# Six last tiles with transfers and PV of their own, and output stores in whole tiles, in a grouped-query attention kernel

## The chip, the core and the metric

One core of a Trainium2 chip. The metric is device time in microseconds (us) of one execution. A profiled execution gives a trace; its "span" runs from the first to the last instruction of the program.

## What is computed

Attention without a mask, 16 batches, 32 query heads over 8 key heads, 16 queries, 2048 keys, head width 128, in bf16:

```
B, Hq, Hkv, Sq, Sk, D = 16, 32, 8, 16, 2048, 128
k = jnp.repeat(k, Hq // Hkv, axis=1); v = jnp.repeat(v, Hq // Hkv, axis=1)
scores = jnp.einsum("bhqd,bhkd->bhqk", q, k) * D ** -0.5
return jnp.einsum("bhqk,bhkd->bhqd", softmax(scores), v)
```

Each of the 128 key heads has 64 query rows. K and V are 64 MB each and are read once; the output is 2 MB.

## The kernel before, in words

**Tiles.** Two key heads make a *tile*: 128 query rows by 2048 keys. There are 64 tiles (0 to 63); two tiles make a *quad* (0 to 31), that is four heads, numbered by g and i. Tile 2d+i holds the two heads (g = 0, 1) of quad d with the same i. A *turn* is four tiles (`STEP`), a *round* eight (`ROUND`).

**One tile's way.** SP (`load_k`) brings K, 1 MB, into one of eight slots of `Kd`. DVE (`kt`) transposes the slot to `KT`. PE (`scores`) writes `S_ps`. DVE scales it to `Sneg` and finds the row bound. ACT (`exp`) writes P and the row sums. PE (`turn_p`) transposes P into `ST_ps`, ACT (`p_out`) copies that to `PT`. PE (`pv`) multiplies by V. P of a quad's two tiles is interleaved, so `pv` works on a quad: two halves of 64 matmuls, each with 64 rows and 64 columns of the array. ACT multiplies the result by the reciprocal of the row sum into `Osb` (DVE does so for the last quads).

**What sets the order.** All transfers go through SP's one queue, written out by hand: for each t from 0 to 70, K of tile t, then stores of an earlier quad, with V of tile p between them where p + `v_lag(p)` = t (a lag of 7 for the late tiles). An instruction that waits holds all behind it. `load_v` waits until PE has finished with the quad that used the buffer before (`sem_pv`; two V buffers of a quad each). `load_k` waits for the transpose of the tile eight before. The V of the last two quads (tiles 60 to 63) goes to slots 0 to 3 of `Kd`, which have no more K by then; that of tiles 62 and 63 is cut in pieces (`LAST_V`). Quads 0 to 27 are stored inside this order, in four transfers of 64 rows each; quads 28 to 31 behind the last V (line 232 on), in two transfers each:

```
    dst = of[d, :, g].rearrange("i x d -> x i d")
    sp.dma_start(dst, Osb[d % NO][64 * g:64 * (g + 1), :, :]).then_inc(sem_o[d % NO], 16)
```

PE, DVE and ACT run loops with the first and last rounds written out; PE's loop has 17 passes (the last for two halves of `pv` alone), and behind it stand the turns of tiles 62 and 63 and the PV of quads 30 and 31.

## Time and profile before

| | |
|---|---|
| median of 3 runs | 343.06 us (342.91 to 343.24) |
| the profiled execution | 342.74 us |
| its span | 340.8 us, so 1.94 us lie around it |
| busy share of the span | DVE 86%, PE 83%, ACT 77% |
| granted PE clock, mean | 0.972 |
| read from HBM, written | 136.31 MB, 2.10 MB |

The profile gives, for each engine, what it did and what ended its idle time; the DMA rows give the share of time in which the 16 DMA engines moved packets, and the rate. The trace further holds a record of each DMA packet (start, duration, size) and of each semaphore increment by a DMA engine, here called a *landing*: every transfer ends with one 4-byte packet on each DMA engine that took part.

### The profile page before, as it was taken

The numbers are of one execution on the slowest core, as the hardware profiler recorded it, in microseconds if no ns is written. First come the engines' busy times: TensorE is split into PE (matmuls) and PEld (weight loads), VectorE is DVE, ScalarE is ACT, GpSimd is POOL, SyncE is SP. The second block draws the span as 40 slices with busy tenths as digits, with TensorE's granted clock in tenths as the row PEclk, the third lists the DMA queues.
The fourth block names the chain that finished last, engine by engine and source line by source line (L and its number), as shares of the span: only waits on it lengthen the run. The fifth ranks groups of instructions, "written<-read, shape, count | busy, mean of one in ns | idle before, by whom it ended". The sixth has DMA issues, their size and how long they took to land.

```text
span 340.8 us, 15409 instructions
## 1 busy us (share of the span) xinstructions
PE 282.6 (83%) x6912; PEld 164.6 (48%) x6912; DVE 293.7 (86%) x265; ACT 261.2 (77%) x349; POOL 31.3 (9%) x22
## 2 busy tenths in 40 slices
PE   1655888888979888998898888988999789897973
PEld 1322445544555455554554554545554544553663
DVE  2999899999989999999989999999999898898611
ACT  2465888888868888988878888888888698787760
POOL 3202020200102020100202020010202010000000
PEclk9857799999999999999999999999999999999998
DMA  7999999999999999999999999999999999999993
GB/s 274 426 418 418 417 418 420 422 420 422 423 423 412 410 425 382 419 422 421 424 421 422 424 422 422 422 422 421 422 423 423 420 423 425 425 420 423 333 414 114
DMA packets 31434, 138.55 MB, mean 407 GB/s; under 512 B 12480, under 2 KB 14784, under 8 KB 15296
## 3 DMA queue, kind: packets, MB, share of 16 engines
q1 hardware_dynamic: 31424, 138.43, 99.2%
q8 instruction: 5, 0.08, 0.1%
q14 instruction: 5, 0.04, 0.0%
HBM read 136.31 MB, written 2.10 MB: 406 GB/s over the span
## 4 chain that ended last, share of the span: by engine, by line
PE 38%; DMA 25%; ACT 20%; issue 7%; DVE 5%; SPq 5%; ACTq 0%
DMA Vd<-in_v_dram 23%; PE S_ps L268 15%; PE ST_ps L279 11%; ACT P L456 11%; PE O_ps L289 10%; ACT PT L465 4%; DVE Sneg L403 3%; ACT O L495 2%; ACT QT L447 2%; SPq L217 2%; DMA Kd<-in_k_dram 2%; DVE KT L395 2%; PE S_ps L289 2%; SPq L183 1%; SPq L202 1%
## 5 line engine op out<-in xcount | busy, mean ns | idle before, releaser
L456 ACT ACTIVATE P<-Sneg,nbias 128x2048 bf16<-128x2048 f32 (+1 forms) x65 | 160.6, 2471 | 4.2 <-DVE Sneg L403 4.2
L403 DVE TENSOR_SCALAR_CACHE_REDUCE Sneg<-S_ps 128x2048 f32<-128x2048 f32 x64 | 145.2, 2269 | 17.5 <-PE S_ps L268 17.4
L395 DVE STREAM_TRANSPOSE KT<-Kd 128x2048 f32<-128x2048 f32 x64 | 147.0, 2298 | 13.6 <-DMA Kd<-in_k_dram 13.6
L268 PE MATMUL S_ps<-KT,QT 32*64 32x512 bf16 x2048 | 127.8, 624 | 21.9 <-DVE Sneg L403 18.9
L465 ACT ACTIVATE PT<-ST_ps 128x512 f32<-128x512 f32 x128 | 69.7, 595 | 55.5 <-PE ST_ps L279 55.5
L279 PE MATMUL ST_ps<-ident,P 128*128 128x128 f32 x512 | 70.2, 281 | 18.5 <-ACT QT L447 10.7
L289 PEld LDWEIGHTS O_ps<-Vd,PT 64*64 64x64 bf16 x3840 | 56.1, 107 | 36.7 <-issue 35.3
L289 PE MATMUL O_ps<-Vd,PT 64*64 64x128 bf16 x3840 | 65.3, 218 | 7.4 <-DMA Vd<-in_v_dram 7.3
L279 PEld LDWEIGHTS ST_ps<-ident,P 128*128 128x128 f32 x512 | 55.3, 142 | 27.7 <-issue 24.0
L268 PEld LDWEIGHTS S_ps<-KT,QT 32*64 32x64 bf16 x2048 | 29.4, 116 | 73.4 <-issue 46.3
L172 POOL COPY Q<-Qn 128x2048 bf16<-128x2048 bf16 x16 | 30.3, 1893 | 250.0 <-PE ST_ps L255 248.8
L255 PEld LDWEIGHTS ST_ps<-ident,Q 64*128 64x128 f32 x256 | 19.2, 145 | 32.1 <-issue 32.1
L255 PE MATMUL ST_ps<-ident,Q 64*128 64x64 f32 x256 | 23.7, 235 | 4.9 <-POOL Q L172 4.9
L447 ACT ACTIVATE QT<-ST_ps 128x512 f32<-128x512 f32 x32 | 19.5, 608 | 9.9 <-PE ST_ps L255 9.8
L495 ACT ACTIVATE O<-O_ps,rrec 128x128 bf16<-128x128 f32 x56 | 17.6, 375 | 0.0
L456 ACT ACTIVATION_READ_ACCUMULATOR P<-Sneg,nbias 128x1 f32 x65 | 13.5, 208 | 0.0
L411 DVE RECIPROCAL rrec<-rowsum 128x1 f32<-128x1 f32 x63 | 10.0, 158 | 0.0
L425 DVE TENSOR_SCALAR O<-S_ps,rrec 128x128 bf16<-128x128 f32 (+1 forms) x4 | 1.3, 347 | 9.0 <-PE S_ps L289 9.0
L289 PE MATMUL S_ps<-Kd,PT 64*64 64x128 bf16 x256 | 5.2, 217 | 2.6 <-issue 2.6
L289 PEld LDWEIGHTS S_ps<-Kd,PT 64*64 64x64 bf16 x256 | 4.6, 107 | 3.3 <-issue 3.3
L509 ACT ACTIVATE O<-S_ps,rrec 64x128 bf16<-64x128 f32 x2 | 0.7, 362 | 6.8 <-PE S_ps L289 6.8
L403 DVE DVE_READ_ACCUMULATOR Sneg<-S_ps 128x1 f32 x64 | 5.3, 83 | 0.0
(10 smaller groups left out, 4.0 us busy)
## 6 DMA issues: line engine op xcount, KB each, us to landing
Kd<-in_k_dram SPq DMA_DIRECT2D x64, 1024.0 KB, 11.1
Vd<-in_v_dram SPq DMA_DIRECT2D x60, 1024.0 KB, 9.5
Qn<-in_q_dram SPq DMA_DIRECT2D x16, 128.0 KB, 9.9
Kd<-in_v_dram SPq DMA_DIRECT2D x2, 1024.0 KB, 8.5
out_dram<-O SPq DMA_DIRECT2D x112, 16.0 KB, 9.2
Kd<-in_v_dram SPq DMA_DIRECT2D x3, 512.0 KB, 9.5
Kd<-in_v_dram SPq DMA_DIRECT2D x1, 256.0 KB, 10.3
out_dram<-O SPq DMA_DIRECT2D x8, 32.0 KB, 5.2
```

Of the source, the lines that this page charges most:

```text
L172: gp.tensor_copy(Q4[:, :, :, :, :].rearrange("p j b r x -> p (j b) r x"), src.unsqueeze(2).to_broadcast([128, 2 * QPAIRS, 4, 64]),).then_i ...
L255: ins = pe.transpose(q_ap()[:, b, 64 * j:64 * (j + 1)], src[rows, j, b, :], ident[rows, rows])
L268: ins = pe.matmul(S_ps[64 * g:64 * (g + 1), 512 * r:512 * (r + 1)], qt[rows, b, e, at:at + 64], kt[rows, b, e, g], start=(acc == 0), stop= ...
L279: ins = pe.transpose(ST_ps[:, 512 * h + 128 * t:512 * h + 128 * (t + 1)], P[w // 2 % NP][:, 128 * y:128 * (y + 1)], ident[:, :])
L289: ins = pe.matmul(o_ap(d, i)[64 * g:64 * (g + 1), :], pt[rows, j % 16 // 2, j % 2, 64 * g:64 * (g + 1)], v_ap(d, g)[rows, j, :], start=(j ...
L395: dve.transpose(KT[u % 2][:, :].rearrange("p (b j a) -> p j b a", b=2, j=J), Kd[:, u % NK, :].bitcast(F32).rearrange("p (j b c) -> p j b c ...
L403: dve.tensor_scalar(Sneg[i % 2][:, :].rearrange("p (j r a) -> p r j a", j=J, r=4), S_ps[:, :].rearrange("p (r j a) -> p r j a", j=J, r=4), ...
L411: ins = dve.reciprocal(rrec[:, x:x + 1], rowsum[:, x:x + 1])
L447: act.activation(QT[x][:, :, :].rearrange("p b (a j) -> p b a j", j=QPAIRS), q_ap().rearrange("p b (j a) -> p b a j", j=QPAIRS), ACT.Copy, ...
L456: act.activation(P[i // 2 % NP][:, :].bitcast(BF16).rearrange("p (n i y e) -> p i n y e", n=n, i=2, e=2)[:, i % 2, lo:hi], Sneg[i % 2][:, ...
L465: ins = act.activation(PT[i % NPT][:, 4 * h:4 * (h + 1), :].rearrange("p t q -> p (t q)"), ST_ps[:, 512 * h:512 * (h + 1)], ACT.Copy,)
L495: ins = act.activation(Osb[y % NO][:, z, :], o_ap(y % NO, z), ACT.Copy, scale=rrec[:, x:x + 1])
```

## The change

The last six tiles (58 to 63, `T0` = 58) leave the scheme of quads.

- V of each goes to slot p - 58 of `Kd`, in rows of 4 KB, as soon as that slot's last K is transposed; the last one in three pieces.
- P of each lies by itself (`alone`), written in two halves; PV of a tile is 32 matmuls of 128 rows by 64 columns (`pv_tile`), into `S_ps` (58 to 61) and `O_ps`.
- The stores of quads 25 to 28 and of the six tiles come behind the last V, one transfer of 32 KB for each tile, by `store_last`, from a second set of output buffers where needed.
- DVE takes one reciprocal for two tiles, and scales all six last tiles.
- PE's loop has 16 passes, and three of its conditions go. `v_lag` falls two tiles later.

```diff
-LAST_V = ((0, 0, 16), (1, 0, 16), (0, 16, 32), (1, 16, 24), (1, 24, 29), (1, 29, 32))
+TILES = 6
+CUTS = (0, 8, 13, 16)
...
     of = out.rearrange("b h s d -> (b h s) d").rearrange("(n g i x) d -> n i g x d", n=ND, g=2, i=2)
+    vt = v.rearrange("b h s d -> (b h s d)").rearrange("(n g i a x) -> n i a g x", n=ND, g=2, i=2, a=128)
...
-        return 2 if p < 2 else 6 if p < 4 else max(VLAG, 11 - (p - 4) // 8)
+        return 2 if p < 2 else 6 if p < 4 else max(VLAG, 11 - max(p - 6, 0) // 8)
...
-    WHOLE = ND - 4
+    WHOLE = ND - 7
...
             def load_v(p):
                 d, g = divmod(p, 2)
+                if p >= T0:
+                    sp.wait_ge(sem_kt[p - T0], ROUNDS)
+                    cuts = CUTS if p == NU - 1 else (0, 16)
+                    for x, (lo, hi) in enumerate(zip(cuts, cuts[1:])):
+                        sp.dma_start(v_tile(p)[:, :, D * lo:D * hi], vt[d, g, :, :, D * lo:D * hi]).then_inc(
+                            sem_vl[x] if p == NU - 1 else sem_vt[p - T0], 16)
                     return
...
+            def store_last(dst, src):
+                sp.add_instruction(mybir.InstDMACopy(
+                    name=nc.get_next_instruction_name(), engine=mybir.EngineType.SP,
+                    ins=sp.lower_ap_dma(src), outs=sp.lower_ap_dma(dst),
+                    queue="qSPDynamicHW", mode="Copy", cce_op=ALU.bypass,
+                )).then_inc(sem_out, 16)
...
+            for d in range(WHOLE, T0 // 2):
+                sp.wait_ge(sem_nm[d % NV], normed(d))
+                for i in range(2):
+                    store_last(of[d, i], o_sb(d)[:, i:i + 1, :])
+            for u in range(T0, NU):
+                d, i = divmod(u, 2)
+                sp.wait_ge(sem_end, u - T0 + 1)
+                store_last(of[d, i], o_sb(d)[:, i:i + 1, :])
...
+            def pv_tile(u):
+                v = v_tile(u).rearrange("p g (j d) -> p g j d", d=D)
+                for j in range(16):
...
+                    for g in range(2):
+                        ins = pe.matmul(
+                            o_tile(u)[64 * g:64 * (g + 1), :],
+                            pt_ap(u)[:, j // 2, j % 2, 64 * g:64 * (g + 1)],
+                            v[:, g, j, :],
...
+            pe.wait_ge(sem_max[STEP - 1], TURNS)
+            pv_tile(NU - 6)
+            pv_tile(NU - 5)
+            pe.wait_ge(sem_exp[2], TURNS)
             pe.wait_ge(sem_po[1], TURNS + 1)
             turn_p(NU - 2)
+            pv_tile(NU - 4)
+            pe.wait_ge(sem_exp[3], TURNS)
             pe.wait_ge(sem_po[2], TURNS)
             turn_p(NU - 1)
+            pv_tile(NU - 3)
+            pe.wait_ge(sem_nm[(T0 // 2 - 1) % NV], normed(T0 // 2 - 1))
+            pv_tile(NU - 2)
+            pe.wait_ge(sem_po[3], TURNS + 1)
+            pv_tile(NU - 1)
...
+                    if at.end and i >= T0 % ROUND:
+                        dve.wait_ge(sem_exp[(i - 2) % STEP], at.tile(i - 2))
...
+                    x = (i - 2) % ROUND
+                    if i % 2 == 0 and (i or at.first) and not (at.end and i > T0 % ROUND):
+                        dve.wait_ge(sem_exp[(i - 1) % STEP], at.tile(i - 1))
+                        dve.reciprocal(rrec[:, x:x + 2], rowsum[:, x:x + 2])
...
+                for h in range(2 if alone else 1):
+                    if alone:
+                        dst = pb[:, J * 64 * (i % 2):J * 64 * (i % 2 + 1)].rearrange("p (t y h e) -> p h t y e", t=n // 2, h=2, e=2)[:, h]
+                        src = sneg.rearrange("p (h t e y) -> p h t y e", h=2, t=n // 2, e=2)[:, h]
```

More of the change, by code (lines that the diff above doesn't have):

```diff
@@ L50, in bass_standalone__gqa_softmax__sampling_kernel @@
     TURNS = NU // STEP
-    assert J == 32 and NU % ROUND == 0 and ROUND == 2 * STEP == NK == 2 * NO and STEP == NPT == 2 * NV
+    T0 = NU - TILES
+    assert TILES % 2 == 0 and TILES <= NK - 2 and J == 32 and NU % ROUND == 0 and ROUND == 2 * STEP == NK == 2 * NO and STEP == NPT == 2 * NV
     scale = float(D) ** -0.5
@@ L68, in bass_standalone__gqa_softmax__sampling_kernel @@
     PT = [sb(f"PT{i}", [128, J // 4, 128], F32) for i in range(NPT)]
-    Osb = [sb(f"O{i}", [128, 2, D], BF16) for i in range(NO)]
+    Osb = [sb(f"O{i}", [128, 2, D], BF16) for i in range(2 * NO)]
     nbias = sb("nbias", [128, ROUND], F32)
-    rowsum = sb("rowsum", [128, ROUND + 1], F32)
+    rowsum = sb("rowsum", [128, 2 * ROUND], F32)
     rrec = sb("rrec", [128, ROUND], F32)
@@ L88, in bass_standalone__gqa_softmax__sampling_kernel @@
     sem_q4 = sem("sem_q4")
-    sem_vl = ring("sem_vl", len(LAST_V) + 1)
+    sem_vt, sem_vl = ring("sem_vt", TILES - 1), ring("sem_vl", len(CUTS) - 1)
+    sem_pe = sem("sem_pe")
     sem_end = sem("sem_end")
-    sem_pe = sem("sem_pe")
     sem_sum = sem("sem_sum")
-    sem_rec = sem("sem_rec")
+    sem_out = sem("sem_out")
     qf = q.rearrange("b h s d -> (b h s) d")
@@ L108, in normed @@
         return d // NV + 2
-    WHOLE = ND - 4
+    WHOLE = ND - 7
+    assert WHOLE + NO <= ND - TILES // 2 < WHOLE + 2 * NO
     store_at = {}
@@ L119, in q_ap, with o_sb, o_ap, o_tile @@
         return ST_ps[:, 0:512].rearrange("p (b x) -> p b x", b=2)
-    def o_ap(d, i):
-        x = 512 * i
-        if d >= ND - 2:
-            return S_ps[:, 1024 * (d % 2) + x:1024 * (d % 2) + x + D]
-        return O_ps[:, x:x + D]
-    def v_ap(d, g):
-        if d >= ND - 2:
-            return Kd[:, 2 * (d % 2) + g, :].rearrange("p (j d) -> p j d", j=J)
-        return Vd[d % NV][:, g, :, :]
+    def o_sb(d):
+        return Osb[d % NO + (NO if WHOLE <= d < T0 // 2 else 0)]
+    def o_ap(i):
+        return O_ps[:, 512 * i:512 * i + D]
+    def o_tile(u):
+        x = u - T0
+        return S_ps[:, 512 * x:512 * x + D] if x < 4 else o_ap(x - 4)
+    def v_tile(u):
+        return Kd[:, u - T0, :].rearrange("p (g x) -> p g x", g=2)
     class Rounds:
@@ L190, in load_v @@
                 d, g = divmod(p, 2)
-                if p >= NU - 2:
-                    if g:
-                        return
-                    sp.wait_ge(sem_kt[3], ROUNDS)
-                    for x, (y, lo, hi) in enumerate(LAST_V):
-                        sp.dma_start(Kd[:, 2 + y, D * lo:D * hi], vf[p + y, :, D * lo:D * hi]).then_inc(sem_vl[1 + x], 16)
+                if p >= T0:
[4 more added lines that the diff above has]
+                            sem_vl[x] if p == NU - 1 else sem_vt[p - T0], 16)
                     return
-                if d == ND - 2:
-                    sp.wait_ge(sem_kt[g], ROUNDS)
-                elif d >= NV and g == 0:
+                if d >= NV and g == 0:
                     sp.wait_ge(sem_pv[d % NV], d // NV)
-                sp.dma_start(v_ap(d, g).rearrange("a j d -> a (j d)"), vf[p]).then_inc(
-                    sem_v[d % NV] if d < ND - 2 else sem_vl[0], 16)
+                sp.dma_start(Vd[d % NV][:, g, :, :].rearrange("a j d -> a (j d)"), vf[p]).then_inc(sem_v[d % NV], 16)
             def load_q(c):
@@ L216, in store @@
                 rows = slice(64 * g, 64 * (g + 1))
-                sp.dma_start(of[d, i, g], Osb[d % NO][rows, i, :]).then_inc(sem_o[d % NO], 16)
+                sp.dma_start(of[d, i, g], o_sb(d)[rows, i, :]).then_inc(sem_o[d % NO], 16)
+            def store_last(dst, src):
[4 more added lines that the diff above has]
+                )).then_inc(sem_out, 16)
             load_q(0)
@@ L231, in _ @@
                     store(d, i, 1)
-            for d in range(WHOLE, ND):
-                for g in range(2):
-                    if d == ND - 1:
-                        sp.wait_ge(sem_end, g + 1)
-                        sp.wait_ge(sem_nm[d % NV], normed(d) + g)
-                    elif g == 0:
-                        sp.wait_ge(sem_nm[d % NV], normed(d))
-                    dst = of[d, :, g].rearrange("i x d -> x i d")
-                    sp.dma_start(dst, Osb[d % NO][64 * g:64 * (g + 1), :, :]).then_inc(sem_o[d % NO], 16)
+            for d in range(WHOLE, T0 // 2):
[6 more added lines that the diff above has]
+                store_last(of[d, i], o_sb(d)[:, i:i + 1, :])
             for s in range(NO):
-                sp.wait_ge(sem_o[s], 64 * (WHOLE // NO) + 32)
+                sp.wait_ge(sem_o[s], 64 * ((WHOLE - s + NO - 1) // NO))
+            sp.wait_ge(sem_out, 32 * (ND - WHOLE))
         @block.tensor
@@ L281, in turn_p, with pt_ap, pv @@
                     ins.then_inc(sem_pt[h][w % STEP], 1)
-            def pv(d, js, gs=(0, 1)):
-                for j in js:
-                    pt = PT[(2 * d + j // 16) % NPT][:, :, :].bitcast(BF16).rearrange("p t (q e) -> p t e q", e=2)
-                    for g in gs:
+            def pt_ap(w):
+                return PT[w % NPT][:, :, :].bitcast(BF16).rearrange("p t (q e) -> p t e q", e=2)
+            def pv(d, half):
+                for j in range(16 * half, 16 * half + 16):
+                    pt = pt_ap(2 * d + half)
+                    for g in range(2):
                         for i in range(2):
@@ L289, in pv @@
                             ins = pe.matmul(
-                                o_ap(d, i)[64 * g:64 * (g + 1), :],
+                                o_ap(i)[64 * g:64 * (g + 1), :],
                                 pt[rows, j % 16 // 2, j % 2, 64 * g:64 * (g + 1)],
-                                v_ap(d, g)[rows, j, :],
+                                Vd[d % NV][rows, g, j, :],
                                 start=(j == 0), stop=(j == J - 1),
@@ L296, in pv @@
                 return ins
+            def pv_tile(u):
+                v = v_tile(u).rearrange("p g (j d) -> p g j d", d=D)
+                for j in range(16):
+                    if u < NU - 1:
+                        if j == 0:
+                            pe.wait_ge(sem_vt[u - T0], 16)
+                    elif j in CUTS:
+                        pe.wait_ge(sem_vl[CUTS.index(j)], 16)
+                    for g in range(2):
+                        ins = pe.matmul(
+                            o_tile(u)[64 * g:64 * (g + 1), :],
+                            pt_ap(u)[:, j // 2, j % 2, 64 * g:64 * (g + 1)],
+                            v[:, g, j, :],
+                            start=(j == 0), stop=(j == 15),
+                            skip_group_check=True,
+                        )
+                ins.then_inc(sem_pe, 1)
             pe.wait_ge(sem_q4, 1)
@@ L304, in _ @@
             pe.wait_ge(sem_qe[1], 1)
-            with pe.Fori(0, TURNS + 1) as it:
+            with pe.Fori(0, TURNS) as it:
                 now = pe.snap(it + 1)
@@ L327, in step_pv @@
                         pe.nop(nofuse=True)
-                    ins = pv(d, range(16 * half, 16 * half + 16))
+                    ins = pv(d, half)
                     if half:
@@ L341, in q_is_out @@
                         pe.wait_ge(sem_qe[i // 2], then)
-                with pe.If(it < TURNS):
-                    step_s(0)
-                    with pe.If(it < TURNS - 1):
-                        step_q(0)
+                step_s(0)
+                with pe.If(it < TURNS - 1):
+                    step_q(0)
                 with pe.If(it >= 2):
                     step_pv(0)
-                with pe.If(it < TURNS):
-                    q_is_out(0)
-                    with pe.If(it >= 1):
-                        step_pt(0)
-                    step_s(1)
+                q_is_out(0)
@@ L354, in _ @@
+                with pe.If(it >= 1):
+                    step_pt(0)
+                step_s(1)
                 with pe.If(it >= 2):
                     step_pv(1)
-                with pe.If(it < TURNS):
-                    with pe.If(it >= 1):
-                        step_pt(1)
-                    step_s(2)
-                    with pe.If(it < TURNS - 1):
-                        step_q(2)
-                    with pe.If(it >= 1):
-                        step_pv(2)
-                    q_is_out(2)
-                    step_pt(2)
-                    with pe.If(it < TURNS - 1):
-                        step_s(3)
-                    with pe.If(it >= 1):
-                        step_pv(3)
-                    step_pt(3)
+                with pe.If(it >= 1):
+                    step_pt(1)
@@ new lines, in _ @@
+                step_s(2)
+                with pe.If(it < TURNS - 1):
+                    step_q(2)
+                with pe.If(it >= 1):
+                    step_pv(2)
+                q_is_out(2)
+                step_pt(2)
+                with pe.If(it < TURNS - 1):
+                    step_s(3)
+                with pe.If(it >= 1):
+                    step_pv(3)
+                step_pt(3)
+            pe.wait_ge(sem_max[STEP - 1], TURNS)
+            pv_tile(NU - 6)
+            pv_tile(NU - 5)
@@ L373, in _ @@
+            pe.wait_ge(sem_exp[2], TURNS)
             pe.wait_ge(sem_po[1], TURNS + 1)
             turn_p(NU - 2)
+            pv_tile(NU - 4)
+            pe.wait_ge(sem_exp[3], TURNS)
             pe.wait_ge(sem_po[2], TURNS)
             turn_p(NU - 1)
-            pe.wait_ge(sem_vl[0], 32)
-            pe.nop(nofuse=True)
-            pv(ND - 2, range(J)).then_inc(sem_pe, 1)
-            for x, (y, lo, hi) in enumerate(LAST_V):
-                if lo == 16 and y == 0:
-                    pe.wait_ge(sem_po[3], TURNS + 1)
-                pe.wait_ge(sem_vl[1 + x], 16)
-                if x == 0:
-                    continue
-                pe.nop(nofuse=True)
-                ins = pv(ND - 1, range(lo, hi), range(2) if x == 1 else [y])
-                if hi == J:
-                    ins.then_inc(sem_pe, 1)
+            pv_tile(NU - 3)
@@ L407, in emit @@
                     ).then_inc(sem_max[i % STEP], 1)
-                    x = (i - 1) % ROUND
-                    if i or at.first:
-                        dve.wait_ge(sem_exp[x % STEP], at.tile(i - 1))
-                        ins = dve.reciprocal(rrec[:, x:x + 1], rowsum[:, x:x + 1])
-                        if at.end and i == ROUND - 1:
-                            ins.then_inc(sem_rec, 1)
+                    x = (i - 2) % ROUND
+                    if i % 2 == 0 and (i or at.first) and not (at.end and i > T0 % ROUND):
+                        dve.wait_ge(sem_exp[(i - 1) % STEP], at.tile(i - 1))
+                        dve.reciprocal(rrec[:, x:x + 2], rowsum[:, x:x + 2])
                     if i + 2 < ROUND or not at.end:
@@ L419, in _, with norm @@
             in_rounds(dve, 1, ROUNDS - 1, emit)
-            def norm(d, parts, rows=slice(0, 128)):
-                dve.wait_ge(sem_o[d % NO], 64 * (d // NO))
-                for i in parts:
-                    x = (2 * d + i) % ROUND
-                    ins = dve.tensor_scalar(Osb[d % NO][rows, i, :], o_ap(d, i)[rows, :], rrec[rows, x:x + 1], None, op0=ALU.mult)
-                ins.then_inc(sem_nm[d % NV], 1)
-            for d in range(WHOLE, ND - 2):
-                dve.wait_ge(sem_pv[d % NV], d // NV + 1)
-                norm(d, range(2))
-            x = ROUND - 1
-            dve.wait_ge(sem_exp[x % STEP], TURNS)
-            dve.tensor_tensor(rowsum[:, x:x + 1], rowsum[:, x:x + 1], rowsum[:, ROUND:ROUND + 1], ALU.add).then_inc(sem_sum, 1)
-            dve.wait_ge(sem_sum, 1)
-            dve.reciprocal(rrec[:, x:x + 1], rowsum[:, x:x + 1]).then_inc(sem_rec, 1)
-            dve.wait_ge(sem_rec, 2)
-            dve.wait_ge(sem_pe, 1)
-            norm(ND - 2, range(2))
-            for g in range(2):
-                dve.wait_ge(sem_pe, g + 2)
-                norm(ND - 1, [1], slice(64 * g, 64 * (g + 1)))
+            def norm(u, src):
+                dst, x = o_sb(u // 2)[:, u % 2, :], u % ROUND
+                return dve.tensor_scalar(dst, src, rrec[:, x:x + 1], None, op0=ALU.mult)
+            d = T0 // 2 - 1
+            dve.wait_ge(sem_pv[d % NV], d // NV + 1)
+            for i in range(2):
+                ins = norm(2 * d + i, o_ap(i))
+            ins.then_inc(sem_nm[d % NV], 1)
+            lo = T0 % ROUND
+            dve.wait_ge(sem_exp[STEP - 1], TURNS)
+            dve.tensor_tensor(rowsum[:, lo:ROUND], rowsum[:, lo:ROUND], rowsum[:, ROUND + lo:2 * ROUND],
+                              ALU.add).then_inc(sem_sum, 1)
+            dve.wait_ge(sem_sum, 1)
+            dve.reciprocal(rrec[:, lo:ROUND], rowsum[:, lo:ROUND]).then_inc(sem_sum, 1)
+            dve.wait_ge(sem_sum, 2)
+            for u in range(T0, NU):
+                d = u // 2
+                dve.wait_ge(sem_pe, u - T0 + 1)
+                if u % 2 == 0:
+                    dve.wait_ge(sem_o[d % NO], 64 * ((WHOLE - d % NO + NO - 1) // NO))
+                norm(u, o_tile(u)).then_inc(sem_end, 1)
         @block.scalar
@@ L450, in q_out, with exp, p_out @@
                 ).then_inc(sem_qe[x], 1)
-            def exp(i, half, count):
+            def exp(i, alone):
                 n = J // 2
-                lo, hi = (0, n) if half is None else (n // 2 * half, n // 2 * (half + 1))
-                sums = ROUND if half else i
-                act.activation(
-                    P[i // 2 % NP][:, :].bitcast(BF16).rearrange("p (n i y e) -> p i n y e", n=n, i=2, e=2)[:, i % 2, lo:hi],
-                    Sneg[i % 2][:, :].rearrange("p (n e y) -> p n y e", n=n, e=2)[:, lo:hi], ACT.Exp,
-                    bias=nbias[:, i:i + 1], scale=-1.0, accum_out=rowsum[:, sums:sums + 1],
-                ).then_inc(count, 1)
-            def p_out(i, n, count=True):
+                pb, sneg = P[i // 2 % NP][:, :].bitcast(BF16), Sneg[i % 2][:, :]
+                for h in range(2 if alone else 1):
+                    if alone:
+                        dst = pb[:, J * 64 * (i % 2):J * 64 * (i % 2 + 1)].rearrange("p (t y h e) -> p h t y e", t=n // 2, h=2, e=2)[:, h]
+                        src = sneg.rearrange("p (h t e y) -> p h t y e", h=2, t=n // 2, e=2)[:, h]
+                    else:
+                        dst = pb.rearrange("p (n i y e) -> p i n y e", n=n, i=2, e=2)[:, i % 2]
+                        src = sneg.rearrange("p (n e y) -> p n y e", n=n, e=2)
+                    ins = act.activation(
+                        dst, src, ACT.Exp, bias=nbias[:, i:i + 1], scale=-1.0,
+                        accum_out=rowsum[:, ROUND * h + i:ROUND * h + i + 1],
+                    )
+                ins.then_inc(sem_exp[i % STEP], 1)
+            def p_out(i, n):
                 for h in range(2):
@@ L468, in p_out @@
                     )
-                if count:
-                    ins.then_inc(sem_po[i % STEP], 1)
+                ins.then_inc(sem_po[i % STEP], 1)
             def emit(at):
                 for i in range(ROUND):
-                    last = at.end and i == ROUND - 1
-                    if last:
-                        p_out(i - TLAG, at.tile(i - TLAG), count=False)
                     act.wait_ge(sem_max[i % STEP], at.tile(i))
-                    if last:
-                        exp(i, 0, sem_po[(i - TLAG) % STEP])
-                        exp(i, 1, sem_exp[i % STEP])
-                        continue
-                    exp(i, None, sem_exp[i % STEP])
+                    exp(i, at.end and i >= T0 % ROUND)
                     if i % 2 == 0 and not (at.end and i >= 4):
@@ L487, in emit @@
                         p_out(i - TLAG, at.tile(i - TLAG))
-                    if i % 2 and (at.first or i >= PVLAG + 1):
+                    if i % 2 and (at.first or i >= PVLAG + 1) and not (at.end and i == ROUND - 1):
                         y = (i - PVLAG - 1) // 2
                         act.wait_ge(sem_pv[y % NV], at.num(2, y // NV + 1))
-                        if at.first >= 2 or (at.first == 1 and y >= 0):
+                        extra = at.end and WHOLE <= ROUND // 2 * (ROUNDS - 1) + y
+                        if not extra and (at.first >= 2 or (at.first == 1 and y >= 0)):
                             act.wait_ge(sem_o[y % NO], at.num(64, 64 * (y // NO)))
@@ L494, in emit @@
                             x = (2 * y + z) % ROUND
-                            ins = act.activation(Osb[y % NO][:, z, :], o_ap(y % NO, z), ACT.Copy, scale=rrec[:, x:x + 1])
+                            ins = act.activation(Osb[y % NO + (NO if extra else 0)][:, z, :], o_ap(z), ACT.Copy,
+                                                 scale=rrec[:, x:x + 1])
                         ins.then_inc(sem_nm[y % NV], 1)
@@ L502, in _ @@
                 p_out(u, TURNS)
-            act.wait_ge(sem_rec, 1)
-            act.wait_ge(sem_o[(ND - 1) % NO], 64 * ((ND - 1) // NO))
-            x = ROUND - 2
-            for g in range(2):
-                rows = slice(64 * g, 64 * (g + 1))
-                act.wait_ge(sem_pe, g + 2)
-                act.activation(Osb[(ND - 1) % NO][rows, 0, :], o_ap(ND - 1, 0)[rows, :], ACT.Copy,
-                               scale=rrec[rows, x:x + 1]).then_inc(sem_end, 1)
 _INS = ['q', 'k', 'v']
```

## The prediction

> **What bounds the kernel now.** I read the page's DMA rows first, then the windows of the last 40 us, then SP's waits and the timeline of the end.

> ```profile
> DMA  7999999999999999999999999999999999999993
> GB/s 274 426 418 418 417 418 420 422 420 422 423 423 412 410 425 382 419 422 421 424 421 422 424 422 422 422 422 421 422 423 423 420 423 425 425 420 423 333 414 114
> ...
> q1 hardware_dynamic: 31424, 138.43, 99.2%
> ```

> The 16 DMA engines are full from start to end at some 422 GB/s; DVE, PE and ACT wait for them. Two places are not full: the slices at 333 and 114. The windows show the first (columns: window, its length, busy time and count by engine, granted clock, DMA share, GB/s):

> ```profile
> 305.00:310.00 5.00, 3.81 (x100) 1.94 (x88) 4.56 (x5) 4.60 (x7) 0.00 (x0) 1.00 1.02 424
> 310.00:315.00 5.00, 4.21 (x116) 2.45 (x120) 4.55 (x5) 2.93 (x5) 0.00 (x0) 1.00 1.03 424
> 315.00:320.00 5.00, 4.36 (x140) 2.56 (x136) 2.95 (x5) 4.59 (x7) 0.00 (x0) 1.00 0.90 342
> 320.00:322.00 2.00, 2.00 (x82) 1.70 (x74) 2.00 (x3) 1.36 (x4) 0.00 (x0) 1.00 1.02 275
> 322.00:324.00 2.00, 1.69 (x56) 1.36 (x45) 0.62 (x3) 1.04 (x3) 0.00 (x0) 1.00 0.99 390
> 324.00:326.00 2.00, 1.02 (x64) 0.96 (x64) 0.00 (x0) 2.00 (x4) 0.00 (x0) 1.00 0.98 402
> ```

> Against 424 GB/s these four windows lose 5·(1-342/424) + 2·(1-275/424) + 2·(1-390/424) + 2·(1-402/424) = 1.9 us. SP's waits and the timeline say why:

> ```profile
> SPq L202 <- PE O_ps L289: 150.2, 28, 10.6
> ```
> ```profile
> 305.84 0.33 SPq L202 DMA_DIRECT2D Vd<-in_v_dram  x1
> ...
> 315.95 0.33 SPq L202 DMA_DIRECT2D Vd<-in_v_dram  x1
> ...
> 317.48 0.59 SPq L202 DMA_DIRECT2D Vd<-in_v_dram  x1
> ...
> 322.47 3.28 SPq L196 DMA_DIRECT2D Kd<-in_v_dram  x6
> ...
> 325.79 13.20 SPq L240 DMA_DIRECT2D out_dram<-O  x8
> ...
> 336.71 1.22 PE L289 MATMUL S_ps<-Kd,PT 64*64 64x128 bf16 x39 [1.81 <-issue]
> ...
> 337.97 0.36 DVE L425 TENSOR_SCALAR O<-S_ps,rrec 64x128 bf16<-64x128 f32 x1 [0.49 <-PE S_ps L289]
> ```

> SP releases two V and two K (4 MB, 9.9 us) each time PE frees a V buffer, every 10 us. At the end there is no K left; the V of tile 58, released at 315.95, comes when the engines run dry. The last V lands between 334.10 and 335.22 (16 landings, mean 334.6; last data packet 334.76), PE ends 337.93, SP issues the last store at 338.40, its last landing is 340.35, the span ends 0.45 later.

> **The change part by part.** Sums are against the profiled execution (span 340.8, 342.74 with 1.94 around it; 0.32 under the median).

> *V of tiles 58 to 63.* They wait for the transposes of tiles 56 to 61, the last of which ends at 302.96 + 2.31 = 305.3, before SP is through its wait for V of tile 56 (305.84). So all six are issued one behind the other, some 0.6 us each, and the engines stay full. The added waits hold up nothing. Of the 1.9 us, 0.2 belong to store packets that run at half rate; 1.7 us go. The 12 stores of quads 25 to 27 also leave the place between the V: 768 packets of 256 B, which follow each other on an engine every 14 ns in the packet records: 768·14/16 = 0.67 us less. Against that, 4 KB packets take 159 ns where 8 KB take 309: five tiles cost 256·159/16 = 2.54 us each in place of 2.47; the last one's three pieces (256 packets each of 84, 55 and 36 ns) 2.80 us; before, the halves and pieces cost 0.26 us over 2.47 per MB. Net 0.4 us more. The last V's data end at a mean engine at 334.6 - 0.46 (last landing behind last packet) - 1.7 - 0.67 + 0.4 = **332.2**.

> *PE, DVE, ACT of the last six tiles.* PV of a tile is 32 matmuls. In the row of 64 matmuls in 1.09 us, each key step takes 55 ns for two row halves and two column halves side by side; with whole rows the two column halves remain: again 1.09 us for 16 steps, or 2 us if they ran one after the other (not taken). V comes every 2.5 us, which hides either. Exp in two halves took 2.83 us (324.26 to 327.09) against 2.72: 0.1 us for five more tiles; the new write pattern (pairs of bf16 eight bytes apart) is not in the trace; between 0 and double, 2.8 us a tile. A tile of a round takes 5 us, which covers the first; the second would delay the last exp by some 5 us. ACT's last copy of PT ended at 330.8 and would end then near 336. As shown below, the end leaves more room than that. 64 reciprocals of 158 ns become 30: DVE waited 13.6 us for K, so nothing comes of it. DVE scales the last tile in 345 ns where a half took 360. Three tests fewer in each of 16 passes, and 192 matmuls fewer: nothing, PE waits for K and V. The later `v_lag` moves a few V by one tile among full engines: nothing.

> *The stores: where I choose.* Behind the last V come 14 transfers of 32 KB (8 for quads 25 to 28, 6 for the tiles), 128 packets of 256 B each. What they cost hangs on how many engines share one. In the packet records each engine's share of a transfer is a run of whole outermost rows closed by a 4-byte packet: 4 packets of 256 B for a store of 64 rows, 8 for the 64 by 2 rows of the last stores, 8 of 8 KB for 128 partitions; 16 landings each. Every transfer of the old kernel lists 64 or 128 rows outermost on both sides; `load_k` lists 64 by 2, the last stores were turned round by `rearrange("i x d -> x i d")`. `of[d, i]` lists g outermost: **2** by 64 by 128, against 128 partitions in the buffer. If shares are cut along the outermost rows there can be two only: 64 packets on each of two engines, 64·14 + 12 = 0.91 us a store, 14 stores one behind the other. The other end is 8 packets on each of 16 engines, 0.12 us. I take 0.91, since every transfer seen is cut so; none with 2 outermost is in the trace.

> [...]

> *The sum.* 332.2 + 14·0.91 = 344.9 for the last packet; 0.37 to its landing (339.98 to 340.35 before), 0.45 to the end of the span: 345.7. With 1.94 around it 347.6, against the median 0.32 more: **347.9 us**, 1.4% slower. The new bound is two DMA engines writing for 13 us while 14 are idle. PE would end near 333.7, ACT and DVE soon after, so all costs above are hidden by some 10 us; that is the cover of exp's pattern too. SP's 14 issues of 0.6 us (8.4 us) stand beside it.

> **Rivals.**

> *Stores over all 16 engines: faster.* Then 13 stores end by 332.2 + 13·0.12 = 333.8. The last V lands at its slowest engine at 335.22 - 2.0 = 333.2; six matmuls and the wait bring PE to 333.7; from PE's end to the span's end it took 2.87 us (337.93 to 340.8): 336.6, that is 338.8 us. For it: nothing forbids it in the trace. Against it: the shares above. It decides whenever a store occupies its engine for less than about (340.8 - 0.82 - 332.2)/14 = 0.56 us. One thing helps it: at 334.7 PE stops for 1.8 us in the middle of a run of matmuls whose data had landed at 333.93, while a 16 KB packet of the queue that the page calls instruction is under way (334.27, 0.95 us). I read it as program code fetched late. The new program's tail has 192 matmuls where the old one had 256, so with their weight loads it is 128 instructions shorter; 39 matmuls and their loads, 78 instructions, stood behind the stop, so it should not meet it again.

> [...]

> *Two engines, but whole rows joined in larger packets.* 64 rows of an output tile are 16 KB in one piece in HBM. At 309 ns for 8 KB a store takes 0.62 us: 332.2 + 8.7 + 0.82 = 341.7, or 343.9 us, hardly a change. Against it: the old stores wrote runs of 1 KB in HBM on each engine and still made 256 B packets.

> *One engine alone.* 14·128·14 ns = 25.1 us: 358.1, or 360.4 us.

> *The gap at 316 stays* (it was not SP's wait but HBM: at 131 to 136 us the rate also falls, to 322 GB/s at the lowest, with the DMA share near 1). Then 1.7 us more on top of the forecast, 349.6. I keep it in the forecast's range.

> **How the numbers follow.** Forecast 0.84, 16 engines 0.11, joined packets 0.03, one engine 0.02. The forecast's own range: down by the two engines' V ending 0.5 early, 13.5 ns a packet (0.5) and a landing spread of the same size, 1.4 lower at most, 346.5; I give 1 us more to what else the full engines may win, 345.5. Up by the gap that stays (1.7), the slowest engine (0.6) and 15 ns a packet (0.9): 351. 345.5 to 351 holds 95 in 100 of the forecast, 0.80 in all. A measurement of this kernel tells about 0.2% (0.7 us) from no change. Faster 0.12 (16 engines), within 0.2% 0.02, slower 0.86.

> **What would show it.** The packets of 256 B at the end: long rows of 64 on two engines for some 13 us, with the DMA share of the last slices near 2/16 and about 35 GB/s; two landings by DMA engines for each of the 14 transfers. The V of tile 58 issued near 307, no slice under 410 GB/s before 332; the last PV near 333.7 with no stop in it, and then DVE, PE and ACT idle for 12 us. Wrong it would be by 16 landings a store and an end near 336.6; the V part would be wrong by a rate under 400 GB/s after 315.

## The result, and the profile after

| | before | changed |
|---|---|---|
| median (range) | 342.99 us (342.30 to 343.24) | 347.38 us (347.08 to 347.46) |
| ratio, 95% interval | | 1.013 [1.011, 1.015] |
| the profiled execution, its span | 342.74 us, 340.8 us | 347.42 us, 345.6 us |

The changed kernel is 1.3% slower; the forecast was 347.9 us and a span of 345.7. First its DMA rows (share of the 16 engines in tenths, then the rate, in 40 slices of 8.64 us).

```profile
DMA  7999999999999999999999999999999999999951
GB/s 262 429 419 412 418 423 419 419 419 425 418 427 420 418 425 421 422 410 421 425 421 424 422 422 423 419 416 425 422 423 421 421 425 420 426 422 417 410 174 31
...
q1 hardware_dynamic: 31868, 138.43, 97.7%
```

The slice of 333 GB/s is gone, and the last two slices are at 174 and 31, where only the last one was low before, at 114. The windows of the end show it more finely (columns as before: window, length, busy time and count of PE, PEld, DVE, ACT, POOL, granted clock, DMA share, GB/s).

```profile
315.00:320.00 5.00, 4.39 (x144) 2.59 (x136) 2.79 (x4) 4.87 (x9) 0.00 (x0) 1.00 1.01 410
320.00:322.00 2.00, 2.00 (x84) 1.74 (x76) 1.81 (x2) 1.69 (x5) 0.00 (x0) 1.00 1.04 416
...
328.00:330.00 2.00, 2.00 (x41) 1.71 (x40) 0.35 (x1) 1.09 (x2) 0.00 (x0) 1.00 1.02 393
330.00:332.00 2.00, 1.13 (x34) 0.95 (x32) 0.54 (x2) 0.00 (x0) 0.00 (x0) 1.00 0.91 308
332.00:334.00 2.00, 1.47 (x32) 1.02 (x32) 0.50 (x2) 0.00 (x0) 0.00 (x0) 1.00 0.25 66
334.00:336.00 2.00, 0.00 (x0) 0.00 (x0) 0.02 (x1) 0.00 (x0) 0.00 (x0) 1.00 0.16 36
336.00:338.00 2.00, 0.00 (x0) 0.00 (x0) 0.00 (x0) 0.00 (x0) 0.00 (x0) 0.56 0.16 36
338.00:340.00 2.00, 0.00 (x0) 0.00 (x0) 0.00 (x0) 0.00 (x0) 0.00 (x0) 0.50 0.16 36
...
344.00:345.00 1.00, 0.00 (x0) 0.00 (x0) 0.00 (x0) 0.00 (x0) 0.00 (x0) 0.50 0.08 19
```

Read it in two halves. From 315 to 322 the rate is 410 and 416 where it was 342 and 275: the dry stretch is closed. From 334 on no engine computes, and the DMA share stands at 0.16 and the rate at 36 GB/s for ten microseconds. The DMA rows of that stretch alone (334 to 344; packets, MB, share of 16 engines):

```profile
q1 hardware_dynamic: 1430, 0.36, 16.0%
```

1408 of the packets have 256 B (the other 22 are the 4-byte ends). 14 ns apart on an engine, they are 19.7 us of work in 10 us: two engines, always full. (The share is a little over 2/16 since the packets' records, 18 ns long, overlap.) The timeline (start, length, engine, line, what ended its idle time) says what runs there and how early the rest is done.

```profile
306.43 15.60 SPq L203 DMA_DIRECT2D Kd<-in_v_dram  x8
322.08 20.28 SPq L225 DMA_DIRECT2D out_dram<-O  x14
...
332.04 1.59 PE L322 MATMUL O_ps<-Kd,PT 128*64 128x128 bf16 x32 [0.26 <-DMA Kd<-in_v_dram]
...
333.67 0.35 DVE L451 TENSOR_SCALAR O<-O_ps,rrec 128x128 bf16<-128x128 f32 x1 [1.50 <-PE O_ps L322]
```

All of the last six V are issued from 306.43 on, one behind the other, where V of tile 58 waited until 315.95 before; in SP's waits that is one wait fewer, 27 in place of 28:

```profile
SPq L208 <- PE O_ps L304: 144.5, 27, 10.2
```

PE ends at 333.63, DVE at 334.02, with no stop in the run of matmuls. The last landing of a store is at 345.13. The landings of the 14 stores show the cause directly: one engine's come at 333.31, 334.22, 335.13, 336.03 and so on to 345.13, another's at 332.78, 333.70, 334.60 and so on to 344.60, both 0.91 us apart on the mean, and no third engine's at all. The semaphore of these stores has 42 updates, three for each: one from each of the two DMA engines, and one that follows each issue's end in SP by 0.42 us (issues that end at 333.29 and 334.18, updates at 333.71 and 334.60); what writes the third, no run shows.

### The profile page after: what moved, and what is told of

It is laid out like the page before. It is cut to its first block, busy times and chain, and to the rows that moved or that the text cites. A ratio compares the mean times of both kernels' runs of the same rounds, so it can differ in the third digit from the quotient of the medians.

```text
span 345.6 us, 14867 instructions
## 1 busy us (share of the span) xinstructions
PE 282.2 (82%) x6720; PEld 164.2 (48%) x6720; DVE 291.5 (84%) x231; ACT 261.6 (76%) x357; POOL 31.3 (9%) x22
## 3 DMA queue, kind: packets, MB, share of 16 engines
q1 hardware_dynamic: 31868, 138.43, 97.7%
## 4 chain that ended last, share of the span: by engine, by line
DMA 37%; PE 30%; ACT 13%; SPq 10%; issue 4%; DVE 3%
DMA Vd<-in_v_dram 28%; PE S_ps L280 13%; PE O_ps L304 9%; PE ST_ps L291 8%; ACT P L491 7%; DMA Kd<-in_k_dram 5%; DMA Kd<-in_v_dram 4%; SPq L203 4%; ACT PT L500 3%; SPq L222 2%; SPq L191 2%; DVE Sneg L433 2%; ACT O L523 1%; ACT QT L476 1%; SPq L208 1%
## 5 line engine op out<-in xcount | busy, mean ns | idle before, releaser
L304 PEld LDWEIGHTS O_ps<-Vd,PT 64*64 64x64 bf16 x3712 | 54.2, 107 | 37.8 <-issue 36.8
L304 PE MATMUL O_ps<-Vd,PT 64*64 64x128 bf16 x3712 | 63.2, 218 | 8.7 <-DMA Vd<-in_v_dram 8.7
L476 ACT ACTIVATE QT<-ST_ps 128x512 f32<-128x512 f32 x32 | 19.4, 606 | 10.7 <-PE ST_ps L267 10.6
L491 ACT ACTIVATION_READ_ACCUMULATOR P<-Sneg,nbias 128x1 f32 x70 | 14.4, 206 | 0.0
L441 DVE RECIPROCAL rrec<-rowsum 128x2 f32<-128x2 f32 x29 | 4.6, 160 | 0.0
L451 DVE TENSOR_SCALAR O<-S_ps,rrec 128x128 bf16<-128x128 f32 x4 | 1.3, 348 | 3.9 <-PE S_ps L322 3.9
L451 DVE TENSOR_SCALAR O<-O_ps,rrec 128x128 bf16<-128x128 f32 x4 | 1.3, 348 | 3.5 <-PE O_ps L322 2.9
L322 PE MATMUL S_ps<-Kd,PT 128*64 128x128 bf16 x128 | 4.1, 221 | 0.0
L322 PEld LDWEIGHTS S_ps<-Kd,PT 128*64 128x64 bf16 x128 | 3.7, 110 | 0.5 <-issue 0.5
```

Of the source, the lines that this page charges most:

```text
L304: ins = pe.matmul(o_ap(i)[64 * g:64 * (g + 1), :], pt[rows, j % 16 // 2, j % 2, 64 * g:64 * (g + 1)], Vd[d % NV][rows, g, j, :], start=(j ...
L476: act.activation(QT[x][:, :, :].rearrange("p b (a j) -> p b a j", j=QPAIRS), q_ap().rearrange("p b (j a) -> p b a j", j=QPAIRS), ACT.Copy, ...
L491: ins = act.activation(dst, src, ACT.Exp, bias=nbias[:, i:i + 1], scale=-1.0, accum_out=rowsum[:, ROUND * h + i:ROUND * h + i + 1],)
```

## The experiments

The theory: the loss is the 14 stores whose outermost dimension is 2, so that two DMA engines write them; the rest of the change, taken together, is a gain. The rival: the loss comes from the stores' new *place* behind the last V, or from something else in the new tail. The kernel before took 342.2 to 343.0 us beside the several groups of runs, so each run is read by its ratio to the kernel before on the same chip. First the changed kernel once more, beside the third group of runs.

> The changed kernel itself, beside the variants of it in this job: 347 us by every theory.

347.16 us, ratio 1.0130 [1.0103, 1.0157].

**The same stores, split along 64 rows.** Only the final loop differs from the changed kernel (it goes by quads, and the last three wait for both their tiles):

```diff
-                    store_last(of[d, i], o_sb(d)[:, i:i + 1, :])
...
-                store_last(of[d, i], o_sb(d)[:, i:i + 1, :])
...
+                for g in range(2):
+                    store_last(of[d, :, g].rearrange("i x d -> x i d"), o_sb(d)[64 * g:64 * (g + 1), :, :])
```

> The changed kernel with its 14 last stores listed as 64 rows by 2 tiles by 128 (one half of a quad each) in place of 2 by 64 by 128; their number, bytes and place behind the last V are the same, the last three quads wait for both tiles. Theory (a transfer is cut along its outermost rows, so the stores ran on two engines): 16 landings a store, the stores of quads 25 to 28 gone within 2 us of the last V, the span 336.6, some 338.8 us against 343.0 before, ratio 0.988. Rival (it is the place of the stores behind the last V that costs, however they are listed): no change from the changed kernel, 347 us.

338.93 us, ratio 0.9913 [0.9898, 0.9927]; again, in another group, as e1b:

> The kernel of sixteen engines once more, beside the two variants of it in this job: 338.9 us by either.

339.28 us, ratio 0.9895 [0.9876, 0.9914]. The same bytes, in as many transfers, in the same place, 64 by 2 by 128 in place of 2 by 64 by 128: by the ratios 7.4 and 8.1 us less than the changed kernel's 1.0130, and the kernel is faster than before. It gains less than the 1.2% expected, 0.87 and 1.05%; the reason stands in the last point on the prediction below. Each store now has 16 landings (224 for 14). The windows of e1b show the tail that went:

```profile
330.00:332.00 2.00, 1.11 (x34) 0.95 (x32) 0.55 (x2) 0.00 (x0) 0.00 (x0) 1.00 1.10 357
332.00:334.00 2.00, 1.47 (x32) 1.01 (x32) 0.46 (x2) 0.00 (x0) 0.00 (x0) 1.00 0.68 150
334.00:336.00 2.00, 0.00 (x0) 0.00 (x0) 0.04 (x1) 0.00 (x0) 0.00 (x0) 0.80 0.25 50
336.00:338.00 2.00, 0.00 (x0) 0.00 (x0) 0.00 (x0) 0.00 (x0) 0.00 (x0) 0.50 0.09 17
```

PE ends as in the changed kernel (333.64), and the last store lands at 337.07 where it landed at 345.13. The rival of the place falls.

**The old kernel with such stores.** The last eight stores of the kernel before, written as two heads outermost. The only other difference is that the last quad's first store now waits for both halves of the quad:

```diff
-                    dst = of[d, :, g].rearrange("i x d -> x i d")
-                    sp.dma_start(dst, Osb[d % NO][64 * g:64 * (g + 1), :, :]).then_inc(sem_o[d % NO], 16)
+                    sp.add_instruction(mybir.InstDMACopy(
...
+                        ins=sp.lower_ap_dma(Osb[d % NO][:, i:i + 1, :]), outs=sp.lower_ap_dma(of[d, i]),
```

> The kernel before with one part alone: its last eight stores listed as 2 by 64 by 128. Theory: two landings a store, eight stores of 0.91 us one behind the other on two engines from 334.2 on: last packet 341.5, span 342.3, 344.5 us, ratio 1.0045. Rival (how they are listed does not count): 343.0 us.

344.46 us, ratio 1.0070 [1.0057, 1.0083], span 342.2. Time and span are as expected, the ratio is not: the kernel before took 342.18 us beside this group, so the loss is 2.4 us where 1.5 (1.0045) were expected, and I can't say where the other 0.9 comes from. Two engines write each store here too (three updates a store), and the price needs nothing else of the change.

**Fewer of them behind the last V.** The changed kernel with quads 25 to 27 stored in the old place, so that 8 two-engine stores are left.

```diff
-    WHOLE = ND - 7
-    assert WHOLE + NO <= ND - TILES // 2 < WHOLE + 2 * NO
+    WHOLE = ND - 4
```

> The changed kernel with quads 25 to 27 stored between the V again, by transfers of 64 rows, so that eight of the 14 stores of 2 by 64 by 128 are left behind the last V. Theory: six stores of 0.91 us less on the two engines, and 0.67 us more for their packets between the V: 347.4 - 5.5 + 0.7 = 342.6 us. Rival (SP's waits put back between the V of tiles 59 and 60 run the engines dry again): 1.7 us more, 344.3 us, with a window under 400 GB/s after 315.

341.92 us, ratio 0.9995 [0.9985, 1.0005]. Six stores fewer make 4.6 us ((1.0130 - 0.9995) · 343), against 6 · 0.91 - 0.67 = 4.8 expected. The rival's dry stretch is not there: from 315 to 330 no window is under 409 GB/s. The loss goes with the count of these stores.

**Four engines.** To see whether the rule is the outermost dimension and not a special case of 2: e1 with quads 25 to 28 in 16 transfers of 4 by 16 by 128.

```diff
...
+                        for i in range(2):
+                            store_last(of[d, i, g].rearrange("(y x) d -> y x d", y=4), o_sb(d)[64 * g:64 * (g + 1), i:i + 1, :])
```

> The kernel of sixteen engines, but the stores of quads 25 to 28 in 16 transfers of one head each, listed as 4 by 16 by 128 in HBM. Theory (shares are cut along the outermost rows): four landings each, 16 packets of 256 B on each of four engines, 16 transfers x 0.23 us = 3.7 us behind the last V, gone by 336; the last quad's stores on those four engines follow at 336, so the span ends some 0.5 us later than with sixteen, 339.5 us. Rival (the number is 16 or 2 whatever the outermost count; or the two inner lists are joined first, as they lie in one piece): 16 landings, no change from sixteen engines, or two landings and 7 us more.

344.15 us, ratio 1.0044 [1.0028, 1.0060]. The split is as expected: 80 updates for 16 transfers, five each, which I read as four engines and one update more, as the stores of two engines have three. The time isn't: I expected 339.5. Its timeline shows the miss:

```profile
321.68 18.75 SPq L225 DMA_DIRECT2D out_dram<-O  x22
```

SP has 22 stores to issue where e1 has 14; three of the early ones were held 2.3, 2.0 and 1.2 us, and from 331.3 on it issues one every 0.56 to 0.70 us without a pause, until 340.42. The last quad was ready in `Osb` at 333.6. The bound was the issuing queue, and I had worked out only what the DMA engines need.

**The wait of V 58 put back.** e1 with the old wait ahead of the V of tile 58 alone.

```diff
+                    if p == T0:
+                        sp.wait_ge(sem_pv[d % NV], d // NV)
                     sp.wait_ge(sem_kt[p - T0], ROUNDS)
```

> The kernel of sixteen engines with one wait put back: V of tile 58 waits again for PE to be through with quad 27, though its buffer is free. Theory (the gap at 316 in the kernel before is SP's wait): the engines run dry at 316 again, V of tile 63 lands 1 to 1.7 us later, 340.2 us. Rival (the gap is HBM's): 338.9 us, no window under 400 GB/s.

340.38 us, ratio 0.9936 [0.9919, 0.9953]; 1.1 us over e1b in the same group. The dry stretch is back, in e9's window:

```profile
315.00:320.00 5.00, 4.30 (x136) 2.47 (x124) 2.79 (x3) 4.87 (x9) 0.00 (x0) 1.00 0.86 309
```

e1b has 407 there. So SP's wait for a V buffer makes such a stretch, and it is not the HBM's. A mean engine's last V lands 0.9 us later than in e1b (333.26 against 332.37). One engine's lands 1.0 after the other fifteen (334.53, the others by 333.49), and PE waits for that one. The slowest of the other fifteen (333.49) is only 0.25 behind e1b's last (333.24), so in these two traces most of PE's delay hangs on one engine; how much of the 1.1 us belongs to it I can't say.

**The stores of quads 25 to 27 alone.** e1 with them between the V, by the same edit of `WHOLE` as above.

> The kernel of sixteen engines with quads 25 to 27 stored between the V, as in the kernel before. Theory (768 packets of 256 B at 14 ns cost the last V 0.67 us): 339.7 us against 339.0. Rival (what costs is SP's wait for quad 27 between the V of tiles 59 and 60): a dry window as well, 340.7 us.

339.13 us, ratio 0.9893 [0.9872, 0.9913], beside e1b's 0.9895 [0.9876, 0.9914]: in time, moving them gains nothing that these runs can tell, where 0.7 us were expected. The V do come a little earlier without the stores between them: a mean engine's last V lands at 332.39 in e7 and at 332.00, 331.99 and 332.04 in e0, e3 and e5c, traces of the same chip with the stores behind; on another chip it is 332.35 in e4 against 331.96 in e1. That is 0.35 to 0.4 us of the 0.67, and the end takes it back: in e1b, SP has six more issues behind the last V, and is late for the last quad: its issues start at 334.46 and 335.11, DVE having finished at 334.04.

**The last issue beside SP.** e1 with one of the last quad's two transfers issued by ACT, which is idle by then.

```diff
...
+                for g in range(2 if d < ND - 1 else 1):
...
+            act.wait_ge(sem_end, TILES)
+            act.dma_start(of[ND - 1, :, 1].rearrange("i x d -> x i d"), o_sb(ND - 1)[64:128, :, :]).then_inc(sem_out, 16)
```

> The kernel of sixteen engines with one of the last quad's two transfers issued by ACT's queue in place of SP's. Theory (the end is now the last tile's way: PE, DVE, issue, landing): the second issue of 0.6 to 0.8 us on SP goes, 338.2 us. Rival (something else ends last): 338.9 us.

338.61 us, ratio 0.9877 [0.9856, 0.9899]: 0.67 less than e1b by the medians, about one SP issue, though the two intervals overlap. Its timeline has the issue 0.04 us after DVE's end (334.36):

```profile
334.40 0.74 ACTq L532 DMA_DIRECT2D out_dram<-O  x1
```

It is the fastest kernel of the study; by medians it beats both the kernel before and the changed one.

**PE's stop.** Three runs test whether PE's 1.8 us stop is late program code. The first puts 100 empty PE instructions at the head of the kernel before.

```diff
+            for _ in range(100):
+                pe.nop(nofuse=True)
             pe.wait_ge(sem_id, 2)
```

> The kernel before with 100 empty instructions at the head of PE's program, where PE waits 4.9 us for Q. Theory (PE's stop of 1.8 us at 334.9 is a block of program code fetched late): every block begins 100 instructions earlier in the work, so the stop leaves the place behind the last V; PE's end falls from 337.9 to some 335.7 and the time to 340.8 us, ratio 0.9935. Rival (the stop is a wait for something else, a landing or a semaphore): 343.0 us, the stop where it was. If the empty instructions take more than PE's first wait, all is later by the rest, up to 1 us.

342.39 us, ratio 1.0013 [0.9997, 1.0029], and the stop where it was, with 39 matmuls left. But the trace has no sign of these instructions, and the same count of PE instructions as before; whether they were in the program at all can't be told. The run says nothing. The second has 50 tiny matmuls and their weight loads instead.

```diff
             pe.wait_ge(sem_id, 2)
+            small = ident[:, :].bitcast(BF16)[0:32, 0:32]
+            for _ in range(50):
+                pe.matmul(O_ps[0:32, 0:32], small, small, start=True, stop=True)
```

> The kernel before with 50 tiny matmuls (32 by 32, a result that is overwritten) at the head of PE's program, where PE waits for Q: with their weight loads 100 instructions that are really in the program. They leave the result alone. Theory (the stop behind 25 matmuls of the last PV is the begin of a block of program code that is fetched late): the stop comes 100 instructions earlier, with 89 matmuls left in place of 39; the last matmuls follow the last landing (335.2) at once, PE ends near 335.7 in place of 337.9, 340.3 us against 342.2, ratio 0.994. Rival (the stop belongs to that place in the work, a landing or a semaphore): it stays with 39 matmuls left, and the time is 342.2 us or a little more.

344.53 us, ratio 1.0055 [1.0036, 1.0074]. The timelines of the end of PE, before and e5b:

```profile
334.02 0.88 PE L289 MATMUL S_ps<-Kd,PT 64*64 64x128 bf16 x25 [0.21 <-issue]
```
```profile
332.56 0.76 PE L292 MATMUL S_ps<-Kd,PT 64*64 64x128 bf16 x40 [0.55 <-issue]
...
336.33 3.33 PE L292 MATMUL S_ps<-Kd,PT 64*64 64x128 bf16 x88 [3.01 <-issue]
```

88 matmuls stand behind the stop where 39 stood: 50 more in front, 49 more behind. The stop is bound to a place in the program, as late code would be, and to no wait. The time I expected (340.3) was wrong, for three reasons that the traces show. One V landing came at 336.21, 1.12 us after the other fifteen, so PE could not have ended near 335.7 in any case. The stop ends 1.3 to 1.5 us after the end of the 16 KB packet in all four kernels that have it: 335.22 to 336.71 before, 334.39 to 335.78 in e2, 335.45 to 336.77 in e5, 334.82 to 336.33 in e5b. The packet moves by less than the stop's begin, so an earlier stop is a longer one, 3.0 us. And behind the longer stop PE runs at half clock, in e5b's windows:

```profile
336.00:337.00 1.00, 0.67 (x26) 0.67 (x27) 0.00 (x0) 0.00 (x0) 0.00 (x0) 0.50 0.03 7
337.00:338.00 1.00, 1.00 (x29) 1.00 (x22) 0.00 (x0) 0.00 (x0) 0.00 (x0) 0.50 0.06 16
338.00:339.00 1.00, 1.00 (x33) 1.00 (x30) 0.08 (x1) 0.00 (x0) 0.00 (x0) 0.51 0.00 0
```

The column before the DMA share is the granted clock: 0.50 until 339, where the kernel before has 1.00 from 336 to 338. The 88 matmuls take 3.33 us; 128 of the same form took 1.98 at full clock.

The third puts 40 such matmuls, by the same lines, at the head of e1, so that the place of the stop comes in the last tile. That is an estimate from counts of instructions: 78 behind the stop in the kernel before, 128 fewer in the new tail, 80 more in front of it here.

> The kernel of sixteen engines with 40 tiny matmuls at the head of PE's program, so that a block of program code begins some 17 matmuls before its end. [...] Rival (the begin of a block in the last tiles costs a stop of 1.8 to 3 us wherever it lies): 341 us or more.

339.62 us, ratio 0.9910 [0.9889, 0.9932], beside e1's 0.9913 [0.9898, 0.9927]: no stop. 16 KB packets come at 329.25 and at 333.74. If the first carries the code of the last matmuls, it ends at 330.34, 1.5 us later (the most between packet and stop's end above) is 331.8, and PE begins the last tile at 332.07: in time. That it is this packet is argued, not shown. If the stops are late code, as e5b suggests, it cost PE 1.8 us in the kernel before and 3.0 us in e5b, and in e5c nothing that the trace shows.

## Why the prediction was right, point by point

- **Two engines, 0.91 us a store.** Right: 0.91 by the landings, and two engines. e1 shows that it is the cut and not the place, e2 that it costs the old kernel too, and e3's five updates a store agree with 4 engines for 4 outermost.
- **The sum of the end.** The last V at the slowest engine was put at 333.2 and came at 333.22, PE's end at 333.7 and came at 333.63, the stores' end at 345.3 (344.9 and 0.37) and came at 345.13, the span at 345.7 and came at 345.6.
- **The V part: the sum held, its terms only in part.** I put 1.7 us on the dry stretch, 0.67 on the moved stores, and 0.4 against them: 2.0 at a mean engine. Between the two profiles a mean engine's last V comes 2.3 us earlier (334.55 to 332.28). Added up over the windows from 315 to 326, what is lost against 424 GB/s falls from 1.9 to 0.3 us. But putting the wait back costs only 0.9 to 1.2 at a mean engine (e9's 333.26 against 332.37 in e1b and 332.09 in e6, on the same chip), and moving the stores brings 0.35 to 0.4. The remaining 0.7 to 1.0 us I can't split, and that the sum came within 0.3 us is in part luck. A sign of what is missing: at 320 to 322 the kernel before falls to 275 GB/s with a DMA share of 1.02, where e9 has 420. I had read this as store packets at half rate, 0.2 of the 1.9 us. By the length of their records, 18 ns, 256 B packets have 0.54 of the rate of 8 KB in 309, and 418 of them start between 315 and 326: 0.2 us; by their distance, 14 ns, it is 0.69 and 0.1 us. The dip is not theirs: the 128 between 320 and 322 take 2.3 of 32 us of engine time. It is V's 8 KB packets that are slow there, 477 ns in the mean of 63; why, is open. The kernel with that wait and with those stores between was not run.
- **No slice under 410 before 332.** By the page's slices it held from the second on: 410 is the lowest up to 328. By the finer windows it did not: 403, 406 and 393 between 322 and 330, and 308 from 330 to 332. To the letter, the last two are the sign that I had named for a wrong V part, a rate under 400 after 315. They are not the old dry stretch: up to 330 the DMA share is 1.01 to 1.04. No 256 B packet starts between 315 and 330; the engines move V in packets of 4 KB, which take 163 ns there (16 · 4096 B / 163 ns = 402 GB/s), and then the smaller ones of the last V. From 330 to 332 the share is 0.91: the engines finish the last V one after another, from 331.58 to 333.22. I had spread the extra time of these packets over the whole and not asked what it makes of a window.
- **exp, PV, DVE.** exp's new write pattern costs nothing: two halves take 1.38 to 1.42 us each, and the old halves took 1.38. (A whole tile's exp takes 2.60 us from start to end; my 2.72 added two records that overlap.) `pv_tile` takes 1.08 to 1.09 us for 32 matmuls where it has its V. Both lie under 12 us of idle engines anyway.
- **PE's stop gone.** Right. e5b supports the reason: the stop shifts by the instructions inserted (100, and 49 more matmuls stand behind it). That its place comes behind PE's end in the new program is worked out (78 instructions stood behind it, and the tail has 128 fewer) and not shown.
- **SP's 14 issues of 0.6 us beside it.** True for the result, but not as put. V's issues took up to 4.1 us where I had put some 0.6, and the first stores' up to 5.2, while the DMA engines were full; the other stores' took 0.82 to 0.99, at the pace of the two engines.
- **The rival of 16 engines, 338.8.** Run as e1 and e1b, its ratios put it at 340.1 and 339.5 on the 343.06 us of the kernel before: the step after PE's end was mis-sized. I took 2.87 us from PE's end to the span's, a row in which one issue follows PE's end; e1b has two (0.65 more) and SP 0.42 late: 2.87 + 1.07 = 3.94, and 333.65 + 3.94 = 337.6, its span. e6 takes one issue away and, by the medians, gets 0.67 back.

## What to carry to other kernels

Look at the outermost dimension of each transfer, on both sides, before you count its bytes: with the same 32 KB, 2 outermost in HBM (against 128 partitions in the buffer) put it on two DMA engines, with landings 0.91 us apart, and 64 on sixteen, with 16 landings a store, and 14 such stores at the end were worth 7 to 8 us, more than all that the change had won. Where transfers are many and small, count the issuing engine's time as well (0.56 to 0.70 us each in e3, one behind the other), above all what must be issued after the last result. When a sum of several terms comes out right, test the terms one by one: here the two that were tested came out smaller than put, and what made up for them is not known.
